# Seven products of a gated layer: four chained in one PSUM bank, weight work in smaller pieces and at other places

## The chip, the cores and the metric

The kernel runs on one core of a Trainium2 chip. The metric is device time in microseconds (us) of one execution. Five engines run their own instruction queues: TensorE multiplies into PSUM (eight banks), VectorE, ScalarE and GpSimd work on tensors in SBUF (here VectorE and ScalarE also read PSUM), and SyncE issues all DMA transfers of this kernel. In the profile they are PE (with PEld, its weight loads), DVE, ACT, POOL and SP.

## The reference

Inputs are fp32: q, k, v of shape (4, 8, 576, 64), decay factors f, and the five weights in float64, which the kernel converts itself by integer operations on the two 32-bit words of each.

```
def _attn_ref(q, k, v, f):                    # cut
    scores = q @ k.T / sqrt(D) + decay of f   # causal, softmax
    return softmax(scores) @ v
def _moe_ref(x, w_in, w_out) -> np.ndarray:   # 2304 x 512, d_ff 2048
    h = np.maximum(x @ w_in, 0.0)
    return (h * h @ w_out).astype(np.float32)
def _moe2_ref(x, w_gate, w_val, w_out):       # d_ff 1536
    gate = 1.0 / (1.0 + np.exp(-(x @ w_gate)))
    val = x @ w_val
    return (gate * val @ w_out).astype(np.float32)
```

The output of attention, heads side by side, goes through `_moe_ref` and then `_moe2_ref`.

## The kernel before

Every large product is made to fp32 accuracy from three TensorE passes: each operand is split into a high part (rounded to `F32R`) by ScalarE (a copy) and a low part (the rest) by VectorE or GpSimd (a subtraction); high x high, high x low and low x high add up in PSUM. Splitting costs ScalarE, VectorE and GpSimd much of their time.

The stages follow each other on TensorE:

1. Attention for 16 pairs of heads, 0 to 196 us. The change does not touch it.
2. Up stage, 196 to 390 us (L693 to L713): x times w_in, 96 groups of 12 matmuls (`up1`, L203), eight banks in turn; ScalarE squares, VectorE makes differences, and DMA stores ("spills", `g_spill`, L198) carry the results out of 14 tiles `gt` to DRAM. Beside it, weights are loaded and converted in "units" (L671 to L681), each in three phases a group apart: `conv_a` (ScalarE), `conv_b` (four VectorE instructions L141, L142, L145, L148), then a use. Six blocks of w_out2 are converted here too and stored to DRAM (`wo_d`). `load_units` (L685) issues the raw loads; there are two raw buffers, so load n + 2 needs the conversion of block n done.
3. w_out stage, 390 to 581 us (L863 to L925): seven products of block sums in place of eight block products, as 84 steps of 12 matmuls. Each step's operand comes back from DRAM (`d_load`) and is split (`d_split`, L664 and L665) two steps ahead. Gate and value blocks of the next stage's first unit are converted beside it (`D1W`). In its last block of products GpSimd makes sums of the result blocks (`t_sum`, L761, `t4_sum`) and ScalarE and VectorE split these (`t_hi`, `t_lo`).
4. Gate and value stage, 581 to 870 us (L1135 to L1146): six units of 256 columns, three pairs of token blocks each (`jj`), and for each pair a gate half and a value half. A half is again seven products (numbered 1 to 7; `product`, L961) of six matmuls of 384 columns. Four results come of them: 1 + 2, 1 + 6 + 5 + 3, 1 + 6 + 7 + 4 and 1 + 6 + 7 + 5. `post` (L988) empties the banks: ScalarE copies product 1, VectorE adds 6, 7, 5 (+3), 7 (+4) in turn into SBUF; products 2, 3 and 4 are accumulated by TensorE onto 1, 5 and 7. Gate results go through a sigmoid on ScalarE, value results are multiplied with them (`gated`) and stored to DRAM. Weights of the next unit are converted beside it; `slot` (L1044) says after which product. `w_sum` (GpSimd), `w_hi` (ScalarE) and `w_lo` (GpSimd, 512, 256 and 1024 columns) make the block sums and the split of a unit's weights.
5. Last stage, 870 to 1022 us (L1158 on): the gated values come back from DRAM and are multiplied with w_out2.

The whole order is written out by hand: inside `tc.manual_schedule()` each engine's queue has its instructions in the order in which the Python code issues them, each engine works its queue in that order, and semaphores make an instruction wait for the data or the buffer that it needs. So the places at which `at`, `D1X` or `TQ1` put a function set the order.

## Time and profile before

Three runs: 1025.5, 1025.58 and 1027.56 us, median 1025.58. The profiled execution took 1024.2 us; its span, from the first to the last instruction, is 1022.3.

| stage | from to, us | PE busy | DVE busy | ACT busy | POOL busy |
|---|---|---|---|---|---|
| up, to its last tenths | 196 to 386 | 190.0 of 190 | 123.2 | 116.4 | 22.4 |
| w_out, before its last block | 420 to 556 | 133.9 of 136 | 112.1 | 76.7 | 53.7 |
| w_out, last block | 556 to 581 | 21.3 of 25 | 19.5 | 10.0 | 18.2 |
| gate and value, start | 581 to 623 | 35.7 of 42 | 38.3 | 17.4 | 28.8 |
| gate and value, later | 623 to 765 | 135.1 of 142 | 117.1 | 45.1 | 54.5 |
| last | 890 to 1000 | 110.0 of 110 | 30.2 | 28.3 | 0.4 |

Matmuls overlap, so "busy" is the time in which at least one is under way; a stage can be 100% busy at different paces. The number of matmuls in a stretch shows the pace.

### The profile page before, as it was taken

The page shows a single profiled execution, that of the slowest core. Times are in us where ns is not written, and L with a number is a line of the kernel's source. Part 1 is how long each engine was busy: PE and PEld are TensorE (multiplying, and loading weights), DVE is VectorE, ACT ScalarE, POOL GpSimd, SP SyncE. Part 2 cuts the span into 40 slices and gives each one's busy share as a digit, 9 for nine tenths or more (in the row PEclk, how much of TensorE's full clock was granted, in tenths as well). Part 3 has the DMA queues.
Part 4 walks back from the last instruction along what each step waited for, and adds up shares of the span by engine and source line. Part 5 has one row for each costly group of instructions (what it writes and reads, how often), then busy time and mean ns, then how long its engine had stood idle before and what let it go on. Part 6 is the DMA issues. An engine that isn't in the chain of part 4 may idle for free. (4 is left out here: it accounts for less than half of the span.)

```text
span 1022.3 us, 16943 instructions
## 1 busy us (share of the span) xinstructions
PE 983.7 (96%) x5968; PEld 914.2 (89%) x5968; DVE 713.9 (70%) x1314; ACT 506.0 (49%) x1037; POOL 349.3 (34%) x403
## 2 busy tenths in 40 slices
PE   7999999999999998999999889999999999999998
PEld 5888878899999998999998779899999999788886
DVE  6878888356666676698788797978787788422221
ACT  6778878566566654554555433322322333322221
POOL 6776777211011122052066874433242322200000
PEclk9999999999999998999999989999999999999999
DMA  5444341177888888766665313223232324533442
GB/s 126 108 124 93 75 91 46 46 240 248 273 282 287 281 251 289 229 206 197 197 180 167 110 37 124 88 88 108 83 119 81 122 88 150 170 134 128 131 135 75
DMA packets 139220, 153.52 MB, mean 150 GB/s; under 512 B 65024, under 2 KB 116224, under 8 KB 139136
## 3 DMA queue, kind: packets, MB, share of 16 engines
q1 hardware_dynamic: 139136, 152.45, 48.7%
q8 instruction: 47, 0.77, 0.3%
q14 instruction: 37, 0.30, 0.1%
HBM read 98.77 MB, written 53.62 MB: 149 GB/s over the span
## 5 line engine op out<-in xcount | busy, mean ns | idle before, releaser
L209 PE MATMUL ps<-xT,hl 128*128 128x384 f32 x1104 | 191.6, 335 | 0.0
L209 PEld LDWEIGHTS ps<-xT,hl 128*128 128x128 f32 x1104 | 191.5, 188 | 0.0
L919 PE MATMUL ps<-gg,ao 128*128 128x384 f32 x1008 | 181.7, 339 | 9.7 <-DVE gg L665 5.9
L919 PEld LDWEIGHTS ps<-gg,ao 128*128 128x128 f32 x1008 | 177.0, 190 | 14.3 <-DVE gg L665 9.9
L665 DVE TENSOR_TENSOR gg<-gl,gg 128x768 fp32r<-128x768 f32 x84 | 94.8, 1139 | 38.7 <-ACT gg L664 38.2
L462 POOL TENSOR_TENSOR pt<-pt,sm 128x128 f32<-128x128 f32 (+2 forms) x142 | 104.3, 766 | 49.1 <-DVE sm L454 43.1
L968 PE MATMUL ps<-xT,r 128*128 128x384 f32 x576 | 114.2, 341 | 3.8 <-POOL r L827 2.8
L968 PEld LDWEIGHTS ps<-xT,r 128*128 128x128 f32 x576 | 102.9, 189 | 4.6 <-POOL r L827 3.1
L664 ACT ACTIVATE gg<-gl 128x768 fp32r<-128x768 f32 x84 | 70.7, 843 | 70.5 <-DMA gl<-g 51.7
L195 DVE TENSOR_TENSOR gt<-gt 128x384 f32<-128x384 f32 x96 | 52.3, 586 | 64.8 <-ACT gt L218 60.0
L359 ACT ACTIVATE pt<-pt,nm 128x128 f32<-128x128 f32 (+1 forms) x144 | 82.5, 583 | 11.2 <-DVE nm L351 11.2
L169 POOL TENSOR_TENSOR hl<-wf,hl 128x512 fp32r<-128x512 f32 x16 | 20.7, 1292 | 161.4 <-ACT hl L165 161.4
L1173 PE MATMUL ps<-f,t 128*128 128x512 f32 x324 | 75.4, 389 | 0.0
L1173 PEld LDWEIGHTS ps<-f,t 128*128 128x128 f32 x324 | 60.8, 188 | 12.6
L1016 ACT ACTIVATE sg<-sg 128x384 f32<-128x384 f32 x33 | 17.4, 526 | 104.2 <-DVE sg L982 103.3
L351 DVE CUSTOM_DVE_ANT_0 pt<-pa,maskc 128x128 f32<-128x128 f32 (+2 forms) x144 | 66.7, 513 | 2.3 <-PE pa L373 2.1
L1125 DVE TENSOR_TENSOR t<-gl,t 128x768 fp32r<-128x768 f32 x24 | 24.4, 1017 | 58.9 <-ACT t L1120 58.9
L968 PE MATMUL ps<-t,r 128*128 128x384 f32 x288 | 57.4, 340 | 5.7 <-DVE sg L982 3.6
L145 DVE SCALAR_TENSOR_TENSOR wtmp<-wraw,wtmp 128x512 int32<-128x512 int32 x68 | 61.3, 901 | 2.0
L982 DVE TENSOR_TENSOR sg<-ps,sg 128x384 f32<-128x384 f32 x94 | 51.8, 553 | 14.7 <-ACT sg L992 5.7
L124 ACT ACTIVATE wtmp<-wraw 128x512 f32<-128x512 f32 x68 | 44.8, 661 | 34.3 <-DMA wraw<-in_moe_w_out_dram 23.8
L968 PE MATMUL ps<-xT,f 128*128 128x384 f32 x288 | 59.1, 342 | 0.0
(180 smaller groups left out, 1804.7 us busy)
## 6 DMA issues: line engine op xcount, KB each, us to landing
gl<-g SPq DMA_DIRECT2D x120, 384.0 KB
g<-gt SPq DMA_DIRECT2D x168, 192.0 KB
wraw<-in_moe_w_out_dram SPq DMA_DIRECT2D x28, 512.0 KB
g<-sg SPq DMA_DIRECT2D x43, 192.0 KB
wraw<-in_moe_w_in_dram SPq DMA_DIRECT2D x16, 512.0 KB
wraw<-in_moe_w_gate_dram SPq DMA_DIRECT2D x12, 512.0 KB
wraw<-in_moe_w_val_dram SPq DMA_DIRECT2D x12, 512.0 KB
g<-pb SPq DMA_DIRECT2D x29, 192.0 KB
```

Of the source, the lines that this page charges most:

```text
L145: lambda: nc.vector.scalar_tensor_tensor(out=xi, in0=hi, scalar=-0x40000000, in1=xi, op0=ALU.bitwise_and, op1=ALU.bitwise_or),
L195: nc.vector.tensor_tensor(out=t, in0=a, in1=b_, op=ALU.subtract)
L209: nc.tensor.matmul(h, lhsT=a, rhs=xT[c][:, b_, t0:t0 + BT], start=(c == 0 and i == 0), stop=(c == KD - 1 and i == 2))
L351: nc.vector.tensor_tensor_reduce(out=o, in0=s, in1=mask, scale=1.0, scalar=3.0e38, op0=ALU.add, op1=ALU.min, accum_out=nm_t[p % 2][:, c:c ...
L359: nc.scalar.activation(out=x, in_=x, func=AF.Exp, bias=nm_t[p % 2][:, c:c + 1], scale=-1.0, accum_out=sm_t[p % 2][:, c:c + 1])
L462: nc.gpsimd.tensor_tensor(out=x, in0=x, in1=sm_t[p % 2][:, c:c + 1].to_broadcast([128, e - a]), op=ALU.mult)
L664: nc.scalar.activation(out=s[:, 0], in_=t, func=AF.Copy)
L665: nc.vector.tensor_tensor(out=s[:, 1], in0=t, in1=s.bitcast(F32)[:, 0], op=ALU.subtract)
L919: nc.tensor.matmul(o, lhsT=ws[:, a, u, cs], rhs=s[:, b_, u, :], start=(k_ in (0, 2, 5) and w == u == x == 0), stop=(w == NW - 1 and u == 1 ...
L968: nc.tensor.matmul(o, lhsT=w[p][:, a, ws], rhs=operand(n, jj, b_, c), start=(n not in (2, 3, 4) and c == x == 0), stop=(c == 1 and x == 2) ...
L982: nc.vector.tensor_tensor(out=out, in0=a, in1=b, op=ALU.add)
L1173: nc.tensor.matmul(o, lhsT=s[:, a, t, cs], rhs=w[b_], start=(u == t == x == 0), stop=(u == NU2 - 1 and t == 1 and x == 2),)
```

## The change

- In the up stage two gate and two value blocks are converted and stored to DRAM in place of the six w_out2 blocks, and come back with `x_load` in the w_out stage. `load_units` is called in phase 2 instead of phase 1. Of w_out2, seven blocks are now converted about the last unit of the gate and value stage, four in its units 1 to 4 (stored, then reloaded), one in the last stage.
- In the w_out stage `t_sum` works on halves (one of two column blocks, 384 columns) and sums, weight splits and block splits stand at other steps (`D1X`). The table of the sigmoid is loaded there by a one-element sigmoid (`warm`).
- In the gate and value stage, products 1, 6, 5 and 3 accumulate in one bank without a break: ScalarE copies the bank after 1, after 6 and after 5, and after 3 it holds the second result. Product 2 has its own bank, 7 and 4 share one. VectorE adds 2 to the copy after 1, (7 + 4) to the copy after 6, and 7 to the copy after 5. Products 3 and 4 of a half are issued in the next half. Sigmoids and the sum with 7 are put into the queues a product later (`todo2`, `follow`).
- A weight's low part on GpSimd comes in pieces of 256 columns, and the fourth piece is new (`w_piece`); first-unit pieces of value and the second unit's gate go to VectorE. `slot` spreads conversion instructions over eight positions of the 14 products of a pair.
- In the last stage two groups of its matmuls stand between the last two products; buffers come from memory freed by the weights.

```diff
...
-        if 1 <= u <= M2 - NE:
-            us.append(("out2", NE + u - 1))
+        if 1 <= u <= 4:
+            us.append((("gate", 0), ("gate", 1), ("val", 0), ("val", 1))[u - 1])
...
             elif ph == 1:
...
+            else:
                 load_units(min(n + 3, NX))
...
-    def t_sum(n, jj):
-        p1, u2, u3 = (pu[n, jj] for n in range(3))
+    def t_sum(n, jj, c):
+        p1, u2, u3 = (pu[i, jj][:, c, :] for i in range(3))
...
+        for b in range(s.start, s.stop, 256):
+            v = slice(b, b + 256)
+            nc.gpsimd.tensor_tensor(
+                out=t[:, 1, v], in0=x[:, b - s.start:b - s.start + 256], in1=t.bitcast(F32)[:, 0, v], op=ALU.subtract
+            )
...
+    for n, (key, m) in enumerate((("gate", 0), ("gate", 1), ("val", 0), ("val", 1))):
+        dx(14 + 4 * n, part_fn(x_load, key, m))
+    for x in range(4):
+        dx(33 + 4 * x, part_fn(w_sum, "gate", 0, x))
+        dx(K6 + 4 if x < 2 else K6 + 5, part_fn(w_sum, "val", 0, x))
+    for x in range(4):
+        dx(K6 + x, part_fn(w_hi, "gate", 0, x))
+        dx(K6 + 1 + x, part_fn(w_lo, "gate", 0, x, nc.vector))
+    dx(K6 + 7, warm)
+    for x in range(6):
+        dx(K6 + 5 + x // 2, part_fn(t_sum, x // 2, 0, x % 2))
+        dx(K6 + 8 + x // 2, part_fn(t_sum, x // 2, 1, x % 2))
...
+    for x, n in enumerate((1, 2, 3)):
+        dx(K6 + 9 + x, part_fn(t_hi, n, 0))
...
-    BANK = {1: 0, 2: 0, 6: 1, 5: 2, 3: 2, 7: 3, 4: 3}
+    BANK = {1: 0, 6: 0, 5: 0, 3: 0, 2: 1, 7: 2, 4: 2}
...
+    def post(key, u, jj, n):
+        o = obank(key, n)
+        if n in (1, 6, 5):
+            t = keep[key, n] = sg()
             nc.scalar.activation(out=t, in_=o, func=AF.Copy)
...
+        if n == 5:
+            t, d = keep.pop((key, 5)), obank(key, 7)
+
+            def c22():
+                add(t, d, t)
+                finish(key, u, jj, 3, t)
+
+            todo2.append([1, c22])
+        elif n in (2, 4):
+            t = keep.pop((key, 1 if n == 2 else 6))
             add(t, o, t)
+            finish(key, u, jj, 0 if n == 2 else 2, t)
+        elif n == 3:
+            if key == "gate":
+                sigm(1, sg(), o)
             else:
+                gated(u, jj, 1, o, keep[1])
+
+    def follow():
+        n = len(todo2)
+        for x in todo2[:n]:
+            x[0] -= 1
+        for x in todo2[:n]:
+            if x[0] < 0:
+                x[1]()
+                todo2.remove(x)
...
-        return u + s // 24, s // 8 % 3, (0, 0, 1, 6, 6, 7, 7, 8)[s % 8]
+    def slot(s):
+        return s // 24, s // 8 % 3, (0, 2, 3, 5, 7, 9, 10, 12)[s % 8]
...
-                seq = [(key, u, jj, n) for n in (1, 6, 7, 5)] + due + [(key, u, jj, 2)]
-                due = [(key, u, jj, n) for n in (4, 3)]
+                x = [(key, u, jj, n) for n in (1, 2, 6, 7, 5)]
+                seq = x[:2] + due[:1] + x[2:4] + due[1:] + x[4:]
+                due = [(key, u, jj, n) for n in (3, 4)]
...
+    for c, x in enumerate(due):
+        down(0, c)
+        follow()
+        product(*x)
+        post(*x)
...
```

TensorE, one gate half of a later unit, before: the operands name the product (`xT` the input's blocks, `t` block sums, `f` and `r` the weights of two keys), and `ps` with its number the bank; products 1, 6, 7, 5, then 4 and 3 of the value half ahead, then 2.

```order
L968 MATMUL ps_2715<-xT_113,r_6556 128x384 x3
L968 MATMUL ps_2715<-xT_114,r_6556 128x384 x3
L968 MATMUL ps_2716<-t_2_6736,r_6556 128x384 x6
L968 MATMUL ps_2718<-t_2_6714,r_6556 128x384 x6
L968 MATMUL ps_2717<-xT_113,r_6556 128x384 x3
L968 MATMUL ps_2717<-xT_114,r_6556 128x384 x3
L968 MATMUL ps_2714<-t_1_6552,r_6889 128x384 x6
L968 MATMUL ps_2713<-xT_115,r_6889 128x384 x3
L968 MATMUL ps_2713<-xT_116,r_6889 128x384 x3
L968 MATMUL ps_2715<-xT_115,r_6556 128x384 x3
L968 MATMUL ps_2715<-xT_116,r_6556 128x384 x3
```

The same place now: products 1, 2, the other half's 3, then 6, 7, the other half's 4, then 5.

```order
L987 MATMUL ps_2719<-xT_117,r_6891 128x384 x3
L987 MATMUL ps_2719<-xT_118,r_6891 128x384 x3
L987 MATMUL ps_2720<-xT_119,r_6891 128x384 x3
L987 MATMUL ps_2720<-xT_120,r_6891 128x384 x3
L987 MATMUL ps_2722<-xT_119,f_6277 128x384 x3
L987 MATMUL ps_2722<-xT_120,f_6277 128x384 x3
L987 MATMUL ps_2719<-t_2_6759,r_6891 128x384 x6
L987 MATMUL ps_2721<-t_2_6792,r_6891 128x384 x6
L987 MATMUL ps_2724<-t_1_6521,f_6278 128x384 x6
L987 MATMUL ps_2719<-xT_117,r_6891 128x384 x3
L987 MATMUL ps_2719<-xT_118,r_6891 128x384 x3
```

Bank 2719 now comes back after two other products each time (1, 6, 5), where each of 1, 6, 7 and 5 had a bank of its own.

GpSimd at the start of the w_out stage's last block of products, before: sums of a value block (L808, `wt`), block sums of 768 columns (L761), then the operations of `t4_sum` on the first pair (L767, L768).

```order
L808 TENSOR_TENSOR wt<-wtmp 128x256 x2
L808 TENSOR_TENSOR wt<-wt,wtmp 128x256
L808 TENSOR_TENSOR wt<-wtmp,wt 128x256
L761 TENSOR_TENSOR pa_4914<-pa_4914,pa_4912 128x768
L761 TENSOR_TENSOR pa_4912<-pa_4912,pa_4910 128x768
L761 TENSOR_TENSOR pa_4910<-pa_4914,pa_4910 128x768
L767 TENSOR_TENSOR pa_4912<-xT_115,pa_4910 128x384
L768 TENSOR_TENSOR pa_4912<-pa_4912,xT_115 128x384
```

And now, from the same value sums on (L815), with the block sums at L768.

```order
L815 TENSOR_TENSOR wt<-wx 128x256 x2
L815 TENSOR_TENSOR wt<-wt,wx 128x256
L815 TENSOR_TENSOR wt<-wx,wt 128x256
L768 TENSOR_TENSOR pa_4900<-pa_4900,pa_4898 128x384 x2
L768 TENSOR_TENSOR pa_4898<-pa_4898,pa_4896 128x384 x2
L768 TENSOR_TENSOR pa_4896<-pa_4900,pa_4896 128x384 x2
```

Six sums of 384 columns stand where three of 768 stood; the next pair's six follow before the operations of `t4_sum`, and the low parts of the value weights, which came after those on GpSimd, are VectorE's.

SyncE at the end of the up stage, before: stores of results (L201), raw loads (L115), the first operands of the w_out stage (L658).

```order
L115 DMA wraw<-in_moe_w_out_dram 128x1024
L201 DMA g_3_61<-gt 128x384 x4
L115 DMA wraw<-in_moe_w_out_dram 128x1024
L658 DMA gl<-g_0_58 128x768
L658 DMA gl<-g_1_59 128x768
L658 DMA gl<-g_2_60 128x768
L201 DMA g_3_61<-gt 128x384
L700 DMA wo_73<-wtmp 128x512
L201 DMA g_3_61<-gt 128x384 x16
```

And now, with the stores at L204, raw loads at L118 and operands at L661.

```order
L118 DMA wraw<-in_moe_w_out_dram 128x1024
L204 DMA g_3_61<-gt 128x384 x4
L661 DMA gl<-g_0_58 128x768
L661 DMA gl<-g_1_59 128x768
L661 DMA gl<-g_2_60 128x768
L204 DMA g_3_61<-gt 128x384
L118 DMA wraw<-in_moe_w_out_dram 128x1024
L204 DMA g_3_61<-gt 128x384 x16
```

The last raw load stands behind the first operands now, and no store of a converted block (L700) is left here.

## Rows read from the trace of the kernel before

**Rows 1.** The page's busy times: us (share of the span) xinstructions.

```profile
PE 983.7 (96%) x5968; PEld 914.2 (89%) x5968; DVE 713.9 (70%) x1314; ACT 506.0 (49%) x1037; POOL 349.3 (34%) x403
```

**Rows 2.** Busy time by stretch: length, then each engine's us (xinstructions), clock, DMA.

```profile
196.00:386.00 190.00, 190.00 (x1097) 190.00 (x1096) 123.19 (x229) 116.38 (x232) 22.38 (x17) 1.00 0.81 259
390.00:392.00 2.00, 0.00 (x0) 0.00 (x0) 1.76 (x3) 1.94 (x5) 1.87 (x2) 1.00 1.07 397
392.00:420.00 28.00, 26.19 (x134) 25.94 (x135) 17.82 (x20) 12.36 (x18) 5.29 (x3) 0.88 0.82 267
420.00:556.00 136.00, 133.92 (x762) 131.66 (x762) 112.11 (x129) 76.70 (x114) 53.71 (x36) 1.00 0.65 190
556.00:581.00 25.00, 21.25 (x115) 19.40 (x114) 19.50 (x20) 9.95 (x14) 18.24 (x12) 1.00 0.50 152
581.00:623.00 42.00, 35.66 (x179) 33.91 (x178) 38.25 (x49) 17.42 (x31) 28.80 (x21) 0.92 0.15 49
623.00:765.00 142.00, 135.09 (x760) 132.65 (x759) 117.08 (x181) 45.13 (x89) 54.48 (x49) 1.00 0.31 99
765.00:830.00 65.00, 63.61 (x362) 63.28 (x362) 51.68 (x81) 20.62 (x41) 20.20 (x17) 1.00 0.28 92
830.00:870.00 40.00, 39.20 (x220) 38.26 (x219) 35.21 (x58) 14.78 (x29) 10.31 (x8) 1.00 0.41 142
870.00:890.00 20.00, 18.73 (x82) 14.83 (x81) 9.09 (x13) 7.14 (x11) 6.19 (x4) 1.00 0.61 197
890.00:1000.00 110.00, 110.00 (x487) 91.09 (x486) 30.15 (x33) 28.28 (x37) 0.36 (x1) 1.00 0.42 136
```

**Rows 3.** What TensorE waited for, whole span: us in total, times, longest us.

```profile
PE ps L968 <- DVE sg L982: 7.1, 5, 2.6
...
PE ps L919 <- DVE gg L665: 5.9, 11, 1.2
...
PE ps L968 <- POOL r L827: 2.8, 1, 2.8
```

**Rows 4.** The same of SyncE's queue, 196 to 396.

```profile
SPq L115 <- DVE wf L148: 41.7, 15, 5.6
```

**Rows 5.** The same of ScalarE, 196 to 396.

```profile
ACT gt L217 <- DMA g<-gt: 3.4, 1, 3.4
```

**Rows 6.** Timeline, 566 to 574: start, us, engine, line [idle <-releaser].

```profile
566.28 6.26 POOL L761 TENSOR_TENSOR pa<-pa,pa 128x768 f32<-128x768 f32 x3
...
568.15 0.84 ACT L782 ACTIVATE f<-pa 128x768 fp32r<-128x768 f32 x1 [3.70 <-POOL pa L761]
...
570.75 2.61 DVE L790 TENSOR_TENSOR f<-pa,f 128x768 fp32r<-128x768 f32 x1
```

**Rows 7.** Groups by form, gate stage (fourth: up stage): xcount | busy, mean ns.

```profile
L982 DVE TENSOR_TENSOR sg<-ps,sg 128x384 f32<-128x384 f32 x94 | 51.8, 553 | 14.7 <-ACT sg L992 5.7 <-PE ps L968 4.5 <-DVE sg L982 0.5
...
L992 ACT ACTIVATE sg<-ps 128x384 f32<-128x384 f32 x22 | 10.5, 478 | 0.6 <-PE ps L968 0.6
...
L145 DVE SCALAR_TENSOR_TENSOR wtmp<-wraw,wtmp 128x512 int32<-128x512 int32 x26 | 30.5, 1173 | 0.7
...
L145 DVE SCALAR_TENSOR_TENSOR wtmp<-wraw,wtmp 128x512 int32<-128x512 int32 x35 | 24.2, 693 | 1.2
...
L827 POOL TENSOR_TENSOR r<-wt,r 128x1024 fp32r<-128x1024 f32 x7 | 18.1, 2581 | 13.4 <-ACT r L823 13.1
...
L808 POOL TENSOR_TENSOR wt<-wtmp 128x256 f32<-128x256 f32 x24 | 19.1, 815 | 49.4 <-DVE wtmp L148 46.4 <-DVE f L827 3.0
```

**Rows 8.** Timeline, 708 to 717, gate stage.

```profile
708.18 2.77 POOL L827 TENSOR_TENSOR f<-wt,f 128x1024 fp32r<-128x1024 f32 x1 [4.38 <-ACT f L823]
...
708.62 2.88 DVE L148 SCALAR_TENSOR_TENSOR wtmp<-wraw,wtmp 128x512 int32<-128x512 int32 x1
...
713.67 1.88 DVE L982 TENSOR_TENSOR sg<-ps,sg 128x384 f32<-128x384 f32 x3
...
716.93 0.53 ACT L1016 ACTIVATE sg<-sg 128x384 f32<-128x384 f32 x1 [7.52 <-DVE sg L982]
```

More of the change, by code (lines that the diff above doesn't have):

```diff
@@ L80 @@
     NU2 = M2 // 2
-    wo_d = [dram.tile([128, 512], F32, name=f"wo_{m}") for m in range(M2)]
+    w_d = {
+        x: dram.tile([128, 512], F32, name=f"w_{x[0]}_{x[1]}")
+        for x in [(key, m) for key in ("gate", "val") for m in range(2)] + [("out2", m) for m in range(M2)]
+    }
     g2_d = [[dram.tile([128, 2, BT], F32, name=f"g2_{u}_{j}") for j in range(6)] for u in range(NU2)]
@@ L968, in product @@
                 nc.tensor.matmul(
-                    o, lhsT=w[p][:, a, ws], rhs=operand(n, jj, b_, c), start=(n not in (2, 3, 4) and c == x == 0),
-                    stop=(c == 1 and x == 2), skip_group_check=n in (2, 3, 4),
-                )
-        return o
-    keep = {}
+                    o, lhsT=w[p][:, a, ws], rhs=operand(n, jj, b_, c), start=(first and c == x == 0),
+                    stop=(c == 1 and x == 2), skip_group_check=not first,
+                )
+    keep, todo2 = {}, []
     def sg():
@@ L1068 @@
+        pos(7 + c, part_fn(t4_sum, 1, c, nc.gpsimd))
+        pos(27 + 2 * c, part_fn(t4_sum, 2, c, nc.vector))
+        for n in range(3):
+            pos(10 + 2 * n + c, part_fn(t_sum, n, 2, c))
+    def slot(s):
+        return s // 24, s // 8 % 3, (0, 2, 3, 5, 7, 9, 10, 12)[s % 8]
     wo = {}
@@ L1083, in o_lo, with o_store @@
         nc.gpsimd.tensor_tensor(out=wo[m][1], in0=cf[m], in1=wo[m][0].bitcast(F32), op=ALU.subtract)
+    def o_store(m):
+        nc.sync.dma_start(out=w_d["out2", m], in_=cf.pop(m))
     def o_load(m):
[L1086 to L1099 removed]
@@ L1100 @@
-    for m in (6, 7):
-        at(NU2 - 1, 2, 5 + 4 * (m - 6), part_fn(o_hi, m), part_fn(o_lo, m), part_fn(o_load, m + 2))
+        t = raw_p.tile([128, 1024], F32, tag="raw", name="wraw")
+        cf[m] = t[:, 0:512]
+        nc.sync.dma_start(out=cf[m], in_=w_d["out2", m])
+    items, mo = [], NE
+    for u in range(NU2):
+        z = 24 * u + (6 if u == 0 else 0)
+        if u == NU2 - 1:
+            items += [(z - 4 + 4 * m, "out2", m) for m in range(NE)]
+            continue
+        for n, key in enumerate(("gate", "val")):
+            items += [(z + 8 * n + 4 * i, key, 2 * u + 2 + i) for i in range(2)]
+        for i in range(min(u, 1)):
+            items.append((z + 16 + 4 * i, "out2", mo))
+            mo += 1
@@ L1119, in e_hi @@
             gg[i] = egg[i % 3]
-            nc.scalar.activation(out=gg[i][:, 0], in_=gl[i], func=AF.Copy)
+            if i > 1:
+                nc.scalar.activation(out=gg[i][:, 0], in_=gl[i], func=AF.Copy)
+                return
+            for c in range(2):
+                nc.scalar.activation(out=gg[i][:, 0, c], in_=gl[i][:, c], func=AF.Copy)
     def e_lo(i):
@@ L1125, in e_lo @@
             nc.vector.tensor_tensor(out=s[:, 1], in0=gl.pop(i), in1=s.bitcast(F32)[:, 0], op=ALU.subtract)
+    for i in range(3):
+        at(NU2 - 1, 2, (1, 2, 7)[i], part_fn(e_load, i))
     for i in range(2):
[L1128 removed]
         at(NU2 - 1, 2, 7 + 3 * i, part_fn(e_hi, i))
         at(NU2 - 1, 2, 9 + 3 * i, part_fn(e_lo, i))
[L1132 to L1133 removed]
+    for x in items[:2]:
+        w_load(*x[1:])
     due = [None, None]
@@ L1161 @@
         e_lo(i + 2)
-        if 8 <= i + 8 < M2:
-            o_hi(i + 8)
-            o_lo(i + 8)
-            o_load(i + 10)
-        s = gg.pop(i)
-        for c in range(3):
-            o = bank(2 + 3 * (j % 2) + c)
-            cs = slice(c * 128, (c + 1) * 128)
-            for t in range(2):
-                w = wo[2 * u + t]
-                for x, (a, b_) in enumerate(((0, 0), (0, 1), (1, 0))):
-                    nc.tensor.matmul(
-                        o, lhsT=s[:, a, t, cs], rhs=w[b_], start=(u == t == x == 0),
-                        stop=(u == NU2 - 1 and t == 1 and x == 2),
-                    )
+        if i < len(rest):
+            m = rest[i]
+            if m == M2 - 1:
+                o_conv0(m)
+                while todo:
+                    one()
+            o_hi(m)
+            o_lo(m)
+            if i + 2 < len(rest):
+                o_load(rest[i + 2])
+        for c in range(2 if i == 0 else 0, 3):
+            o = down(i, c)
             if u == NU2 - 1:
```

248 lines of the change are left out of this document (112 added, 136 removed).

## The prediction, made before the changed kernel was run

> **What bounds the kernel now.** I read the page's busy shares first: TensorE is busy for 983.7 of 1022.3 us [rows 1]. That share hides pace, so I cut the span into stages and counted matmuls per stretch [rows 2]. The stretch 196 to 386 runs without a gap: 1097 matmuls of 384 columns in 190.0 us, 0.1732 us each. That is the pace against which I measure the stages that the change touches; a stretch's loss is its length less its matmuls times 0.1732.
>
> - 390 to 420 (start of the w_out stage): 2.0 us with no matmul, then 28.0 - 134 x 0.1732 = 4.8; loss 6.8
> - 420 to 556: 136.0 - 762 x 0.1732 = 4.0
> - 556 to 581 (its last block of products): 25.0 - 115 x 0.1732 = 5.1
> - 581 to 623 (start of the gate and value stage): 42.0 - 179 x 0.1732 = 11.0
> - 623 to 765: 142.0 - 760 x 0.1732 = 10.4; 765 to 830: 2.3; 830 to 870: 1.9
> - 870 to 890 (start of the last stage): the pace there is that of 890 to 1000, 110.0 / 487 = 0.2259 us; 20.0 - 82 x 0.2259 = 1.5
>
> Together 43.0 us: all that a better order can win. Before 196 and after 890 nothing moves on TensorE, and 196 to 386 has no loss to win. The table of waits says who is late: mostly VectorE, whose adds empty PSUM (L982) or whose subtractions make operands (L665), once GpSimd's weight subtraction (L827) for 2.8 us [rows 3]. The granted clock adds to the loss: a mean of 0.88 in 392 to 420 and 0.92 in 581 to 623, part of each at the lower of its two levels (1.2 and 2.4 GHz) after TensorE stood, against 1.00 around them [rows 2].
>
> **The change, part by part.**
>
> *Raw loads a group later, w_out2 blocks out of the up stage.* In 196 to 396 SyncE's queue stands 41.7 us, up to 5.6 at a time, in front of a w_out load whose buffer VectorE's last conversion instruction still reads (L148) [rows 4]; the stores of results queue behind. Near the end ScalarE waits 3.4 us for a result tile that such a store must free [rows 5]; the operands of the w_out stage's first steps are behind it in ScalarE's queue, and TensorE stands at 390. Now the load is queued one group (12 matmuls, 2.08 us) after the conversion instead of with it. Four gate and value blocks take the place of six w_out2 blocks, so two 512 KB loads and two 256 KB stores leave this stretch, and none of the four falls in its last quarter; ScalarE and VectorE are busy 116.4 and 123.2 of 190.0 us there, which covers the conversions. If a late load instead makes ScalarE wait, eight PSUM banks of queued results stand before TensorE does. Bounds 0 to 6.8 us; I take 4.8, leaving 2.0, because DMA shows share 1.07 at 390 to 392 and the last steps' stores still burst. The first rows of the next stage need three loads of 384 KB, and they stay in the same place of the queue.
>
> *Conversions out of the w_out stage.* 16 VectorE instructions go from 400 to 556. GpSimd's four sums for a gate block are spaced by four steps instead of standing in front of an operand sum. Bounds 0 to 4.0; I take 2.0, since the operand sums of 512 columns that GpSimd and VectorE both touch stay as they are.
>
> *Block sums in half pieces, issued before their readers.* At 566.28 GpSimd takes 6.26 us for three sums of 768 columns; ScalarE, which has the next split in the same step, stands 3.70 us for the first; VectorE's subtraction of 128x768 beside it takes 2.61 us [rows 6]. Now the first reader on ScalarE stands three to four steps (over 6 us) behind its sums, and the chain on GpSimd up to the stage's end is 4 + 12 shorter sums: at 0.82 each for 256 columns [rows 7] and half of 2.09 for 384, 3.3 + 12.5 = 15.8 us, from 16.7 us (eight steps) before the end. The value weights' low parts, for which TensorE stood 2.8 us [rows 3], are made by VectorE instead, five and more products ahead of their use. Bounds 0 to 5.1 at 556 to 581; I take 3.6. For 581 to 623, 0 to 11.0; I take 7.5: it is the stage's start and all the operand preparation still falls into it.
>
> *Four products chained in one bank.* Per half (gate or value of one token pair, 36 in all) VectorE makes 3 sums instead of 5: 72 fewer, at 0.553 us [rows 7], 39.8 us. ScalarE makes 72 more copies at 0.478 us, 34.4 us, in a stage where it is busy 17.4 + 45.1 + 20.6 + 14.8 = 97.9 of 289 us [rows 2]; it ends near half busy. But VectorE (38.3 + 117.1 + 51.7 + 35.2 = 242.3 of 289 us) gets back five w_out2 conversions of four instructions in this stage, at most 0.693 to 1.173 each [rows 7], so 14 to 23 us, and about 5 us of weight and block sums that GpSimd had. It stays near 80 to 85% busy over a shorter stage. What changes is who waits. In the old order five conversion instructions stood together: VectorE was held from 708.62, where one took 2.88 us beside GpSimd's 2.77 us subtraction of 1024 columns, to 713.67, when three late sums start, and the sigmoid came at 716.93 [rows 8]. Now conversion instructions stand at eight separate positions per token pair, at most one per product, and 1024 columns on GpSimd become four pieces. TensorE needs, between links of the chain, one copy: two other products (12 matmuls, 2.08 us) lie between, and the copy takes 0.48.
>
> The price of the cut on GpSimd: one 1024-column piece at 2.58 becomes four of about 0.82 [rows 7], 3.3 us; at 54.5 busy of 142 that is covered.
>
> The conversion instruction of L145 takes 0.693 us in the up stage and 1.173 in the gate stage, where GpSimd works beside it [rows 7]. The Trainium skill (SBUF — State Buffer, "Who interferes with whom") says that a VectorE instruction with two SBUF inputs and a GpSimd instruction that reads SBUF exclude each other for a whole instruction, whoever issues first; the 2.88 beside 2.77 agrees. By that rule shorter pieces shorten each hold, but not their sum, and the cut would win lateness alone: the sum is the same as below.
>
> For 623 to 870 the bounds are 0 and 14.6 us; a loss here or in 581 to 623 is possible through ScalarE's queue alone, and is the second rival. The other terms take work off a queue or move it earlier, so their lower end is 0. If all of it ran as 765 to 830 does (2.3 us lost in 65), 247 x 2.3 / 65 = 8.7 would remain and 5.9 be won; with half that loss 10.2. I take 8.
>
> *Last stage.* Two groups of its matmuls stand between the last two products, and the third split buffer is free earlier: of 1.5 us I take 1.0; ends 0 and 1.5.
>
> **Sum.** 4.8 + 2.0 + 3.6 + 7.5 + 8.0 + 1.0 = 26.9 us. The profiled execution took 1024.2 us (span 1022.3 and 1.9 around it); 1024.2 - 26.9 = 997.3. The median of the runs shown, 1025.58, is 1.4 above the profiled one: 999.
>
> **Rivals.**
>
> *VectorE stays late (25%).* Its load hardly falls, as worked out. If lateness follows load, the gate stage from 581 wins 5 instead of 15.5 us, and the time is 999 + 10.5 = 1009. For it: the busy share. Against: the lump at 708 to 714 is order, not load, and 765 to 830 runs at 0.1796 us per matmul under the same share (51.7 of 65).
>
> *ScalarE's queue blocks the chain; slower (9%).* The sigmoid that follows product 2 waits for VectorE's sum and stands in front of the copy after product 6, which product 5 needs. From product 2's end to product 5 lie four products, 4.2 us at 1.05; less 0.53 for the sigmoid and 0.48 for the copy, VectorE's sum may end up to 3.2 us after its product. Beyond that TensorE waits. ScalarE's 7.52 us wait for VectorE at 716.93 [rows 8] shows that such lateness exists. If every half loses 1 us so, 36 us are added, the gate stage's 15.5 are not won, and the first 11.4 stay: 1025.6 - 11.4 + 36, less the 20 us of old stalls that these replace, about 1030. The Trainium skill (PSUM — Partial Sum Buffer, "Engine vs sequencer instructions") has ScalarE's queue as strictly in order; the row agrees, and by that rule this rival needs nothing but a late sum. I hold it unlikely because an add stands at most behind one conversion instruction now.
>
> *Nothing comes free (4%).* Each stall is replaced by another of its size, as DMA in 390 to 420 and operand work in 581 to 623 would have it: within 2 us of 1025.6.
>
> *Nearly all goes (7%).* Only 3 or 4 of the 43.0 us stay: 986.
>
> **How the numbers follow.** The forecast, 999 (992 to 1006 by its own terms), has 55%. A change of 0.2%, 2 us, is about what a measurement of this kernel can tell. Faster: 55 + 25 + 7, and a point of the slower rival, whose stalls may be smaller than the rest wins: 88%. Same: 4%. Slower: 8%. The range 988 to 1013 takes in the forecast with its bounds, most of the 1009 case, and leaves out the slower cases and most of the 986 case.
>
> **What would show it.** Right: 390 to 400 without a gap and at clock 1.00; SyncE no longer waiting for L148; no wait of ScalarE for block sums at the stage's end; matmul pace from 623 on under 0.179; VectorE sums 108 instead of 180, copies 108 instead of 36. Wrong: TensorE waiting for ScalarE's copies at the third or sixth product of a half, or the late VectorE sums still ending most of its waits, or a new wait for raw blocks by ScalarE in 196 to 386.

## The result, and the profile after

The changed kernel takes 1000.33 us (median of four runs, 1000.02 to 1000.61), the kernel before beside it 1026.57 (1025.5 to 1029.05): ratio 0.9741, 95% interval 0.9721 to 0.9761. The profiled executions are 24.0 us apart (1024.2 and 1000.19), where the prediction's sum was 26.9.

The page's busy times after [rows 1]: us, share of the span, instructions.

```profile
PE 975.2 (98%) x5968; PEld 911.2 (91%) x5968; DVE 663.2 (66%) x1254; ACT 544.2 (55%) x1124; POOL 353.6 (35%) x439
```

VectorE does 50.7 us less, ScalarE 38.2 more. Busy time by stretch after [rows 2], with the same columns; the borders follow the stages, which now end earlier (the w_out stage at 570.8 instead of 581.2).

```profile
386.00:388.00 2.00, 2.00 (x13) 2.00 (x13) 1.97 (x3) 0.94 (x3) 1.20 (x1) 1.00 0.57 206
...
390.00:392.00 2.00, 1.11 (x7) 1.08 (x7) 2.00 (x2) 1.90 (x4) 2.00 (x3) 1.00 0.54 148
392.00:420.00 28.00, 26.54 (x151) 25.81 (x150) 19.33 (x24) 13.58 (x19) 1.98 (x2) 1.00 0.72 214
420.00:548.00 128.00, 126.98 (x728) 125.70 (x727) 95.82 (x106) 69.05 (x99) 51.51 (x35) 1.00 0.67 193
548.00:572.50 24.50, 24.23 (x138) 23.59 (x137) 21.02 (x24) 14.71 (x23) 17.79 (x14) 1.00 0.59 172
572.50:614.50 42.00, 35.78 (x186) 34.01 (x185) 41.21 (x54) 20.50 (x42) 28.96 (x23) 0.92 0.17 54
614.50:750.00 135.50, 134.85 (x766) 134.20 (x765) 94.19 (x161) 64.99 (x135) 57.42 (x70) 1.00 0.37 121
750.00:815.00 65.00, 65.00 (x371) 65.00 (x371) 44.95 (x76) 32.58 (x67) 26.84 (x31) 1.00 0.39 128
815.00:846.00 31.00, 31.00 (x177) 30.91 (x176) 23.61 (x39) 16.06 (x34) 5.75 (x5) 1.00 0.45 150
846.00:866.00 20.00, 20.00 (x92) 16.84 (x91) 10.30 (x14) 7.41 (x12) 7.51 (x6) 1.00 0.59 193
```

With the pace of 0.1732 us per matmul the losses are these (in the last stretch 12 of the 92 matmuls are of the gate and value stage, 80 at the last stage's 0.2259; the "first 42 us" of the gate and value stage are 572.5 to 614.5 after, from 1.7 us into it):

| stretch | loss before | loss after | won | predicted |
|---|---|---|---|---|
| 390 to 420 | 6.8 | 30 - 158 x 0.1732 = 2.6 | 4.2 | 4.8 |
| w_out, middle | 4.0 | 1.9 | 2.1 | 2.0 |
| w_out, last block | 5.1 | 0.6 | 4.5 | 3.6 |
| gate and value, first 42 us | 11.0 | 42 - 186 x 0.1732 = 9.8 | 1.2 | 7.5 |
| gate and value, later | 14.6 | 2.8 + 0.7 + 0.3 = 3.8 | 10.8 | 8.0 |
| border to the last stage | 1.5 | 0 | 1.5 | 1.0 |

One trace stands behind each row. Where runs below leave a stage's order as it is in the changed kernel, their traces show how far executions differ: 180.2 to 182.7 us for the w_out stage, 272.9 to 274.8 for the gate and value stage. So a row is good to about 2 us.

The sum won is 24.3. One row is far off: the start of the gate and value stage hardly gained. Before, TensorE stood 2.8 us there for GpSimd's low part [rows 3] and 3.5 for VectorE's sums; both waits are gone, and others of the same size are there. What TensorE waited for after, 571 to 620 (total, times, longest, in us):

```profile
PE ps L987 <- DVE f L797: 4.2, 2, 3.4
PE ps L987 <- ACT f L789: 1.8, 1, 1.8
PE ps L987 <- ACT sg L1020: 0.3, 1, 0.3
```

The timeline of the same place after: start, length, engine, line, in brackets the idle time before and its releaser.

```profile
557.79 2.10 POOL L815 TENSOR_TENSOR wt<-wx 128x256 f32<-128x256 f32 x2 [5.80 <-ACT gg L667]
...
562.08 16.54 POOL L768 TENSOR_TENSOR pa<-pa,pa 128x384 f32<-128x384 f32 x12
...
582.82 1.19 POOL L775 TENSOR_TENSOR pa<-pa,xT 128x384 f32<-128x384 f32 x1
...
584.05 0.84 ACT L789 ACTIVATE f<-pa 128x768 fp32r<-128x768 f32 x1 [4.18 <-POOL pa L775]
584.94 0.44 PE L987 MATMUL ps<-f 128*128 128x384 f32 x1 [1.80 <-ACT f L789]
585.31 1.75 DVE L797 TENSOR_TENSOR t<-pa,t 128x768 fp32r<-128x768 f32 x1
586.98 1.75 DVE L797 TENSOR_TENSOR f<-pa,f 128x768 fp32r<-128x768 f32 x1
588.78 1.97 PE L987 MATMUL ps<-f 128*128 128x384 f32 x5 [3.40 <-DVE f L797]
```

GpSimd begins the four sums of a value block (L815) at 557.79, 13.0 us before the stage's end, after standing 5.8 us, and works from 562.08 for 16.54 us on twelve block sums (the first and the second token pair's), and only then makes the sums for product 4 of the first pair (L774, L775). ScalarE, then VectorE, then TensorE wait for these one after the other; after the 3.40 us TensorE runs some 13 matmuls at 320 ns, the lower clock level, and the stretch has a mean granted clock of 0.92.

### The profile page after: what moved, and what is told of

Read it like the earlier page. It is cut to its first block, busy times and chain, and to the rows that moved or that the text cites. A ratio compares the mean times of both kernels' runs of the same rounds, so it can differ in the third digit from the quotient of the medians.

```text
span 998.4 us, 16960 instructions
## 1 busy us (share of the span) xinstructions
PE 975.2 (98%) x5968; PEld 911.2 (91%) x5968; DVE 663.2 (66%) x1254; ACT 544.2 (55%) x1124; POOL 353.6 (35%) x439
## 4 chain that ended last, share of the span: by engine, by line
PE 82%; DVE 7%; ACT 3%; DMA 3%; issue 2%; POOL 2%; SPq 0%; ACTq 0%; DVEq 0%; POOLq 0%
PE ps L987 23%; PE ps L212 19%; PE ps L1204 15%; PE ps L934 10%; PE pa L510 4%; PE pa L376 4%; PE pa L476 3%; DMA gl<-g 2%; PE pa L340 2%; PE pa L447 1%; DVE gg L668 1%; DVE ao L653 1%; ACT gg L667 1%; PE pa L212 1%; PE pa L482 1%
## 5 line engine op out<-in xcount | busy, mean ns | idle before, releaser
L934 PE MATMUL ps<-gg,ao 128*128 128x384 f32 x1008 | 177.6, 335 | 3.6 <-DVE gg L668 3.4
L934 PEld LDWEIGHTS ps<-gg,ao 128*128 128x128 f32 x1008 | 174.5, 188 | 6.7 <-DVE gg L668 6.4
L987 PE MATMUL ps<-xT,r 128*128 128x384 f32 x576 | 110.5, 342 | 0.7 <-ACT sg L1020 0.4
L667 ACT ACTIVATE gg<-gl 128x768 fp32r<-128x768 f32 x84 | 70.9, 845 | 71.1 <-DMA gl<-g 38.0
L1020 ACT ACTIVATE sg<-ps 128x384 f32<-128x384 f32 x65 | 31.9, 491 | 55.2 <-PE ps L987 54.2
L220 ACT ACTIVATE gt<-ps 128x384 f32<-128x384 f32 x92 | 44.5, 484 | 27.3 <-PE ps L212 25.1
L1000 DVE TENSOR_TENSOR sg<-ps,sg 128x384 f32<-128x384 f32 x65 | 36.0, 556 | 34.9 <-PE ps L987 27.2
L127 ACT ACTIVATE wtmp<-wraw 128x512 f32<-128x512 f32 x68 | 45.0, 663 | 24.7 <-DMA wraw<-in_moe_w_out_dram 8.2
L987 PE MATMUL ps<-xT,f 128*128 128x384 f32 x288 | 57.4, 342 | 0.3 <-ACT sg L1020 0.3
L987 PE MATMUL ps<-t,r 128*128 128x384 f32 x288 | 54.7, 337 | 0.0
```

The source lines that it names most:

```text
L127: nc.scalar.activation(out=x, in_=rf[:, :, 1], func=AF.Abs)
L220: nc.scalar.activation(out=r, in_=uph.pop(g), func=AF.Relu)
L667: nc.scalar.activation(out=s[:, 0], in_=t, func=AF.Copy)
L934: nc.tensor.matmul(o, lhsT=ws[:, a, u, cs], rhs=s[:, b_, u, :], start=(k_ in (0, 2, 5) and w == u == x == 0), stop=(w == NW - 1 and u == 1 ...
L987: nc.tensor.matmul(o, lhsT=w[p][:, a, ws], rhs=operand(n, jj, b_, c), start=(first and c == x == 0), stop=(c == 1 and x == 2), skip_group_ ...
```

## The experiments

Theory at the outset: late raw loads took away the gap at 390; spread conversions, the chain (products 1, 6, 5 and 3 in one bank) and short GpSimd pieces together took the late VectorE sums away; the order on GpSimd's queue makes the new stall at 585. The rivals are in the expectations.

**Product 4's first sum ahead**, and the splits of the second and third pair some products later.

```diff
-        dx(K6 + 8 + x // 2, part_fn(t_sum, x // 2, 1, x % 2))
         ...
         dx(K6 + 11, part_fn(t4_sum, 0, c, nc.gpsimd))
+    for x in range(6):
+        dx(K6 + 11, part_fn(t_sum, x // 2, 1, x % 2))
...
-        (1, 1, 4, 6), (2, 1, 7, 9), (3, 1, 11, 13), (4, 1, 17, 19),
+        (3, 1, 9, 11), (1, 1, 11, 13), (2, 1, 13, 15), (4, 1, 20, 22),
...
-        pos(7 + c, part_fn(t4_sum, 1, c, nc.gpsimd))
+        pos(14, part_fn(t4_sum, 1, c, nc.gpsimd))
...
```

> The changed kernel, with one thing moved: GpSimd makes the two sums for product 4 of the first token pair before the six sums of the second pair, and the splits of the second and third pair stand a few products later in the order that follows. Theory (order on GpSimd's queue): the changed kernel's two waits at 584.94 (1.95 us) and 588.78 (3.66 us), and the slow matmuls until about 593.5, come from product 4's sum standing behind twelve others (16.54 us). Then both go, the loss of the 42 us at the start of the gate and value stage falls from 9.8 to about 4, and the time from 1000.3 to 993.5-996. Rival (too much operand work at the stage's start for ScalarE and VectorE, whatever the order): the wait moves to an operand of the second pair, the loss stays above 8, and the time is 999-1002.

Measured: 996.88 us (996.32 to 997.3), ratio 0.9706 (0.9683 to 0.9729), 3.5 us under the changed kernel. First 42 us and the stretch after:

```profile
572.50:614.50 42.00, 36.02 (x193) 33.53 (x194) 41.69 (x56) 21.84 (x44) 29.09 (x23) 1.00 0.19 62
614.50:750.00 135.50, 135.34 (x771) 135.02 (x771) 94.76 (x162) 64.90 (x136) 57.56 (x70) 1.00 0.37 123
```

The clock stays at 1.00 and no wait is over 1.7 us. But the loss is still 42 - 193 x 0.1732 = 8.6, not 4: VectorE is busy 41.7 of 42 and ends 4.2 us of smaller waits, ScalarE 1.6. The long stall was order, as the theory has it. The size of the theory's win was wrong: the loss stays above 8, as the rival said, and the time lies between the ranges of the two. Of the 3.5 us the table's measure finds 1.2 in these 42 us.

**Second unit's gate blocks out of the stage's start**, without and with the edit above.

```diff
-        if 1 <= u <= 4:
-            us.append((("gate", 0), ("gate", 1), ("val", 0), ("val", 1))[u - 1])
+        if u <= 5:
+            us.append((("gate", 0), ("gate", 1), ("val", 0), ("val", 1), ("gate", 2), ("gate", 3))[u])
...
+    for i in range(2):
+        pos(2 * i, part_fn(x_load, "gate", 2 + i))
```

> The changed kernel with the two gate blocks of the second unit converted in the up stage (its six blocks now in units one to six of eight) and read back from DRAM at the start of the gate and value stage, so that eight conversion instructions, some 8 to 9 us of VectorE, leave the first 42 us of that stage, where VectorE is busy 41 of 42. The order of the sums and splits is that of the changed kernel. Theory (too much work on VectorE there is what keeps the stage's start lossy): TensorE's two long waits shrink to under 2 us together, the clock stays up, loss 4 to 5 instead of 9.8, time 994-996.5; less 0 to 1 for the block that now falls late in the up stage. Rival (GpSimd's order, the sum for product 4 behind twelve others, decides): the waits at 585 and 589 stay within 1 us of 5.6 together, 999-1001.

> Both: product 4's first sum ahead on GpSimd as in the first run of this series, and the two gate blocks of the second unit converted in the up stage. Theory (order on GpSimd and load on VectorE each cost part of it): the start of the gate and value stage loses 3 to 4 us instead of 8.6, time 991-993.5. Rival (one of the two suffices, or the load is only moved to the up stage's end): no better than 996.9 by more than 1, 995.9-998.

Measured: 1003.97 us without (1001.32 to 1005.18; ratio 0.9789, 0.9773 to 0.9806), 999.26 with (0.9737, 0.9722 to 0.9751). Both are slower than either expectation allowed. The same stretch, first without, then with:

```profile
572.50:614.50 42.00, 35.77 (x186) 34.29 (x186) 33.45 (x45) 20.09 (x39) 29.12 (x24) 0.92 0.07 24
```

```profile
572.50:614.50 42.00, 38.11 (x211) 36.19 (x210) 37.57 (x46) 21.79 (x42) 32.59 (x27) 1.00 0.09 33
```

Without the first edit VectorE is busy 33.5 of 42 instead of 41.2, and TensorE waits as long as in the changed kernel, to the tenth of a microsecond:

```profile
PE ps L987 <- DVE f L797: 4.2, 2, 3.4
PE ps L987 <- ACT f L789: 1.8, 1, 1.8
```

So load alone is not the cause of the long stall. With both edits the loss is 42 - 211 x 0.1732 = 5.5, and the whole stage, up to the first group of the last stage, runs from 575.13 to 844.48, 269.4 us, against 570.75 to 845.5, 274.8, in the changed kernel; with the first edit alone it takes 272.4, with this one alone 273.6. So once the order is right, load is the next limit. The total is no better than with the first edit alone. Six blocks instead of four are now converted in the up stage; TensorE waits 2.1 us at 391.8 and 3.4 at 395.6, and 390 to 420 loses 30 - 127 x 0.1732 = 8.0, where the first edit alone loses 3.2. Without the first edit, in the same up stage, the profiled execution loses 4.2 there. It is the fastest of its four, only 1.1 us above the changed kernel's; the other 2.5 us of the median are in no trace. All six blocks in the first five units, with both edits, was not tried.

**Further moves of the splits**: product 4's first split earlier, the third pair's sums ahead of the second pair's product-4 sum, the third pair's splits in another order. The diff is against the first run of this series.

```diff
-    pos(8, part_fn(t_hi, 4, 0))
-    pos(10, part_fn(t_lo, 4, 0))
+    pos(6, part_fn(t_hi, 4, 0))
+    pos(8, part_fn(t_lo, 4, 0))
...
-        pos(14, part_fn(t4_sum, 1, c, nc.gpsimd))
+        pos(17, part_fn(t4_sum, 1, c, nc.gpsimd))
...
-            pos(15 + 2 * n + c, part_fn(t_sum, n, 2, c))
+            pos(11 + 2 * n + c, part_fn(t_sum, n, 2, c))
```

> The changed kernel with product 4's first sum moved ahead on GpSimd as in the first run of this series, and beyond it: the low part of product 4's operand stands on VectorE ahead of three adds, GpSimd makes the third pair's sums before the second pair's product-4 sum, and the splits of the third pair follow in the order in which their sources are free. Theory (the remaining waits at 584.87, 1.4 us, and 608.62, 1.9 us, are order in VectorE's and GpSimd's queues): both go, 993-995. Rival (VectorE is full from 570 to 615, and a split that is moved ahead makes another one late): 996-998.

Measured: 998.74 us (0.974, 0.9726 to 0.9755), a miss: the two waits are gone, and others of 1.6 and 2.4 us stand at 590.7 and 593.5, the second for a split of the second pair. Such new waits are what the rival said, but the time lies beyond its range too. The first 42 us:

```profile
572.50:614.50 42.00, 37.62 (x201) 36.13 (x200) 41.73 (x54) 20.88 (x41) 30.22 (x23) 0.96 0.17 54
```

Here the loss falls from 8.6 to 7.2, and the whole stage takes 271.9 us instead of 272.4. What is lost lies in front of it: the w_out stage, which has the same instructions in both runs, took 182.7 us in this trace and 180.2 in the other. So whether these moves cost or gain is not settled.

**Old order of the products, all else changed.** `SLOT`, `BANK`, `post` and the product sequence are those of before.

```diff
-                x = [(key, u, jj, n) for n in (1, 2, 6, 7, 5)]
-                seq = x[:2] + due[:1] + x[2:4] + due[1:] + x[4:]
-                due = [(key, u, jj, n) for n in (3, 4)]
+                seq = [(key, u, jj, n) for n in (1, 6, 7, 5)] + due + [(key, u, jj, 2)]
+                due = [(key, u, jj, n) for n in (4, 3)]
```

> The changed kernel with the products of a half in their order of before, with the banks and the emptying of before (five VectorE sums per half instead of three, one copy instead of three) and without the two groups of the last stage between the last products; the spread conversions, the short GpSimd pieces and the late raw loads stay. Theory (what the chain takes from VectorE's path to TensorE is worth most of the gate and value stage's 11.6 us): late VectorE sums end TensorE's waits again, 6 to 10 us come back in that stage and 1 in the last, time 1007-1012. Rival (spreading the conversions over eight positions is what did it): the sums come in time in the old order too, time 1000-1004.

Measured: 1003.54 us (0.9773, 0.9745 to 0.9801), 3.2 more than the changed kernel. Two later stretches of the stage:

```profile
614.50:750.00 135.50, 135.00 (x768) 134.68 (x768) 106.33 (x196) 49.96 (x99) 59.01 (x70) 1.00 0.36 118
750.00:815.00 65.00, 65.00 (x371) 65.00 (x370) 49.57 (x93) 24.23 (x48) 26.57 (x31) 1.00 0.40 128
```

VectorE has 12.1 us more to do from 614.5 to 750 (106.3 against 94.2), and TensorE does as many matmuls (768 against 766). The rest is at the borders: 1.9 us of standing at 850.9, where the two groups of the last stage that this edit also takes out stood, and 177 matmuls instead of 186 in the first 42 us. So with the conversions spread the chain as such is worth little; the rival was right.

**Conversions in lumps, all else changed.**

```diff
-        return s // 24, s // 8 % 3, (0, 2, 3, 5, 7, 9, 10, 12)[s % 8]
+        return s // 24, s // 8 % 3, (0, 0, 1, 7, 7, 8, 8, 9)[s % 8]
```

> The changed kernel with the conversion instructions of the gate and value stage in lumps, at the positions 0, 0, 1, 7, 7, 8, 8, 9 of the 14 products of a pair instead of 0, 2, 3, 5, 7, 9, 10, 12. Theory (the chain tolerates a late VectorE, since only copies of ScalarE stand between its links): TensorE hardly notices, 1000-1003. Rival (the spreading is what did it): five conversion instructions of 0.7 to 1.2 us stand in VectorE's queue before a sum, products wait for their bank, and 5 to 9 us of the stage's 11.6 come back, 1005-1010.

Measured: 1011.46 us (0.9847, 0.9823 to 0.9871), 11.1 more than the changed kernel, beyond even the rival's range; the theory (the chain makes TensorE indifferent) falls. First what VectorE waited for, 572 to 870, then the worst place:

```profile
DVE wtmp L144 <- ACT wtmp L127: 11.2, 14, 2.3
```

```profile
584.49 0.84 ACT L789 ACTIVATE f<-pa 128x768 fp32r<-128x768 f32 x1 [4.18 <-POOL pa L775]
585.24 0.65 ACT L127 ACTIVATE wtmp<-wraw 128x512 f32<-128x512 f32 x1
...
585.92 0.85 DVE L144 TENSOR_SCALAR wtmp<-wtmp 128x512 f32<-128x512 f32 x1 [2.31 <-ACT wtmp L127]
586.69 1.01 DVE L1000 TENSOR_TENSOR sg<-ps,sg 128x384 f32<-128x384 f32 x2
...
587.38 0.66 PE L987 MATMUL ps<-f 128*128 128x384 f32 x1 [3.80 <-DVE sg L1000]
```

The first conversion instruction (L144) needs ScalarE's copy (L127). In the changed kernel the copy is issued one of the eight positions ahead, one or two products; with this table it falls on the same product for half of the blocks, as here. So the edit does two things: it makes lumps, and it takes that distance away. ScalarE is held by GpSimd's late sum, VectorE by ScalarE, the sums behind L144 by VectorE, and TensorE by the bank that they must empty. The changed kernel shows no such wait of L144 among VectorE's waits of that stretch; the kernel before has 10.0 us of it. TensorE also waits 4.2 us in the stage for ScalarE's copies of the banks (L1020), up to 1.6 at a time.

Of the 11.1 us, 4.8 fall in the first 42 us (158 matmuls, loss 14.6 instead of 9.8). Later:

```profile
614.50:750.00 135.50, 133.89 (x752) 130.62 (x751) 95.59 (x162) 62.68 (x134) 54.54 (x68) 1.00 0.35 115
750.00:815.00 65.00, 63.92 (x363) 62.96 (x362) 43.14 (x75) 29.74 (x64) 24.80 (x32) 1.00 0.38 125
```

With 0.9 from 815 to 846 (174 matmuls) and 1.7 from there to the stage's end at 857.4 (56) the loss is 5.3 + 2.1 + 0.9 + 1.7 = 10.0, more than the changed kernel's 3.8 and less than the 14.6 of the kernel before. So with lumps, too, other parts of the change win some 5 us of the later stage. Whether it is the chain was not separated: the chain alone, in the kernel before, was not run.

**The table of positions alone, in the kernel before.**

```diff
-        return u + s // 24, s // 8 % 3, (0, 0, 1, 6, 6, 7, 7, 8)[s % 8]
+        return u + s // 24, s // 8 % 3, (0, 2, 3, 5, 7, 9, 10, 12)[s % 8]
```

> The kernel before with one thing of the change: the conversion instructions of the gate and value stage at the positions 0, 2, 3, 5, 7, 9, 10, 12 of the 14 products of a pair instead of 0, 0, 1, 6, 6, 7, 7, 8. Theory (the spreading is most of what the gate and value stage won, as the two runs of the changed kernel with the old products, 3.2 us, and with lumps, 11.1 us, say): the stage takes 278 to 281 us instead of 288.7, ratio 0.990 to 0.993. Rival (with five VectorE sums per half VectorE is full, and the spreading helps only together with the chain or with short pieces on GpSimd): 0.996 to 1.000.

Measured: ratio 0.9928 (0.9904 to 0.9953), 1017.71 us. The stage takes 279.9 us (584.15 to 864.03) instead of 288.7. Two stretches [rows 2]:

```profile
581.00:623.00 42.00, 35.21 (x180) 33.60 (x178) 38.28 (x48) 16.75 (x29) 32.88 (x22) 0.92 0.15 49
623.00:765.00 142.00, 141.18 (x801) 140.48 (x801) 113.51 (x190) 48.46 (x92) 53.31 (x50) 1.00 0.32 105
```

From 623 to 765 there are 801 matmuls instead of 760, a loss of 142 - 801 x 0.1732 = 3.3 instead of 10.4, with VectorE busy 80% of it (82% before). This one line is 8.8 us of the stage's gain; the first 42 us gain nothing from it. In both kernels the copy (L124) and the first conversion instruction (L141) stand at one and the same product, so here the spreading acts alone. VectorE's wait for the copy in the whole stage, first before, then with the table:

```profile
DVE wtmp L141 <- ACT wtmp L124: 10.0, 11, 1.2
DVE wtmp L141 <- ACT wtmp L124: 5.9, 8, 1.2
```

More than half of that wait stays, while TensorE's waits for VectorE's sums from 640 on fall from 9.0 to 1.6 us. So the lump behind the wait hurt more than the wait itself.

**Long GpSimd pieces, all else changed.**

```diff
-        for b in range(s.start, s.stop, 256):
-            ...
+        nc.gpsimd.tensor_tensor(out=t[:, 1, s], in0=x, in1=t.bitcast(F32)[:, 0, s], op=ALU.subtract)
```

> The changed kernel with GpSimd's work in long pieces again: a weight's low part in 512, 256 and 1024 columns, the block sums of the first and later pairs in 768 columns. Theory (a long GpSimd instruction holds VectorE's next instruction back for as long as it runs, and that makes it late): VectorE instructions of 2 us and more beside them, 3 to 6 us lost, 1003-1006, most of it at 556-623. Rival (GpSimd and VectorE share the same sum of time whatever the pieces, and TensorE no longer depends on VectorE within 2 us): within 1.5 us of 1000.3.

Measured: 1000.22 us (0.9738, 0.9713 to 0.9763), the changed kernel's time. VectorE's L148 from 623 to 840, first with long pieces, then in the changed kernel (xcount, busy, mean ns, idle):

```profile
L148 DVE SCALAR_TENSOR_TENSOR wtmp<-wraw,wtmp 128x512 int32<-128x512 int32 x26 | 24.0, 924 | 0.4
```

```profile
L148 DVE SCALAR_TENSOR_TENSOR wtmp<-wraw,wtmp 128x512 int32<-128x512 int32 x26 | 18.3, 702 | 0.4
```

The holds are there (the longest L148 takes 2.24 us beside long pieces, 0.76 beside short ones), and they cost TensorE nothing. The cut into pieces was not part of the gain.

**Raw loads early, in the changed kernel; raw loads late, in the kernel before.**

```diff
             elif ph == 1:
...
-            else:
                 load_units(min(n + 3, NX))
             if ph < 2:
```

```diff
             elif ph == 1:
...
+            if ph == 2:
                 load_units(min(n + 3, NX))
```

> The changed kernel with the raw weight loads of the up stage queued in phase 1 again, one group of 12 matmuls earlier, with the conversion instead of after it. Theory (SyncE's stand before the conversion's last instruction is what kept TensorE waiting at 390 before the change): SyncE waits over 60 us for VectorE's L148 and L151 in 196 to 396 again, ScalarE waits for a result tile at the stage's end, and 3 to 5 us come back at 390 to 420; 1003-1005. Rival (what helped there is that the two last units of loads and four transfers are gone from the up stage's end): no wait at 390, 1000-1001.

> The kernel before with one thing of the change: the raw weight loads of the up stage are queued one group later (phase 2); the six w_out2 blocks stay in this stage. Theory (the place of the loads decides): the two gaps at 390 to 400 shrink to 1 us each and 3 to 5 us are won, ratio 0.995 to 0.997. Rival (the number of blocks near the stage's end decides): the gap of 2.0 us with no matmul stays, ratio 0.999 to 1.001.

Measured: 999.57 us (0.9746, 0.9732 to 0.9761) and ratio 1.0017 (1.0 to 1.0033): on both sides the loads' place is worth nothing. What SyncE's queue waited for in 196 to 396, first with early loads, then in the changed kernel:

```profile
SPq L118 <- DVE wf L151: 28.3, 9, 5.1
SPq L113 <- DVE wf L151: 27.3, 12, 4.0
```

```profile
SPq L113 <- DVE wf L151: 24.4, 12, 3.2
SPq L118 <- DVE wf L151: 20.6, 9, 3.8
```

So early loads wait 55.6 us for VectorE's L151, late ones 45.0, and TensorE starts the w_out stage alike (155 and 158 matmuls from 390 to 420).

**Blocks at the end of the up stage**: two more in the changed kernel; the six of the kernel before in earlier units.

```diff
-        if 1 <= u <= 4:
+        if 1 <= u <= 6:
```

```diff
-        if 1 <= u <= M2 - NE:
-            us.append(("out2", NE + u - 1))
+        for x in ((0,), (1, 2), (3,), (4,), (5,), (), (), ())[u]:
+            us.append(("out2", NE + x))
```

> The changed kernel with two more weight blocks (gate 2 and 3) loaded, converted and stored in the last quarter of the up stage, as the kernel before had two w_out2 blocks there; their stored values are not used, so this is work in addition. Theory (the blocks that no longer fall near the up stage's end, and their two loads of 512 KB and stores of 256 KB, are what took the gap at 390 away; the place of the loads was not, as two runs showed): DMA share stays above 1.0 to 392, TensorE stands 2 to 4 us more at 390 to 400 with some 3 us at the lower clock, 1003-1006. Rival (the gap went for another reason, the order of the queues at the border of the stages): within 1 us of the changed kernel, 999.5-1001.5.

> The kernel before with the six w_out2 blocks of the up stage in its first five of eight units (one each, two in the second) instead of units two to seven: the same work, none of it in the last quarter. Theory (blocks near the stage's end make the gap at 390): 390 to 420 loses 2 to 3 us instead of 6.8 and keeps the higher clock, 3 to 5 us won, ratio 0.995 to 0.997. Rival (the gap depends on something else): ratio 0.999 to 1.001.

Measured: 1005.64 us (0.9806, 0.9791 to 0.982), 5.3 more; and ratio 0.9964 (0.9952 to 0.9976), 3.7 us less than before. With two more blocks:

```profile
390.00:392.00 2.00, 0.60 (x4) 0.28 (x2) 1.90 (x5) 1.94 (x6) 0.00 (x0) 1.00 1.03 377
392.00:420.00 28.00, 23.91 (x123) 23.66 (x124) 20.20 (x22) 12.74 (x19) 7.09 (x4) 0.88 0.66 207
```

The gap is back, with DMA at share 1.03 and the clock at 0.88, as before the change [rows 2]: loss 30 - 127 x 0.1732 = 8.0 against 2.6. In the other run the profiled execution shows less than its times: 390 to 420 loses 30 - 141 x 0.1732 = 5.6 instead of 6.8, at a clock of 0.94, and that execution is the slowest of its six; where the rest of its 3.7 us comes from stays open. So it is the blocks, not the place of the loads. Their number and their place are not separated, and the gap differs between executions: the two runs with the second unit's gate blocks share one up stage, and their traces lose 4.2 us with DMA at share 0.50 in 390 to 392, and 8.0 with DMA at 1.01.

## Why the prediction held, and where it failed

- **Start of the w_out stage (4.8, measured 4.2).** The size held, the cause did not. The step gave the win to the later raw loads and SyncE's 41.7 us in front of them [rows 4]; with L110's 19.9 they were 61.6 us, fell only to 45.0, and were harmless. The win came from what the same step named second, the blocks: fewer of them, and none in the stage's last quarter. Which of the two counts was not separated.
- **w_out, middle and last block (2.0 and 3.6, measured 2.1 and 4.5).** The sizes came out within what one trace can tell. ScalarE's wait of 3.70 us for the block sums [rows 6] is a wait of 2.44 at 570.43 now. Long sums gave the same time, so it is not the half pieces; that the earlier place of the sums and the 16 instructions fewer did it is argued, not shown.
- **Start of the gate and value stage (7.5, measured 1.2).** This step failed, and the term that failed is GpSimd's chain of 4 + 12 sums: 15.8 us, from 16.7 us before the w_out stage's end, so done 0.9 us before it. It began 13.0 us before the end and took 20.8 us (557.79 to 578.62), so it was done 7.9 us behind it. The twelve alone took 16.54, at 1.38 us each instead of half of 2.09. The wait of 5.8 us in front of the chain was in no term; the trace puts it down to ScalarE (L667), but the one buffer of `wt` was also read by VectorE (L836) until 557.65, and which it was is not shown. The step also stopped at the stage's end and did not follow product 4's sum, behind the twelve, to its reader. With the step's own figures that would have shown no stall: product 4's operand ready some 7 us into the stage (an estimate: 5.4 for its sums and 2.6 for its splits in the trace after, less 0.9), where TensorE asks for it 12.4 us in. So the sizes decided. Moving that sum ahead took the stall away and 3.5 us of the time; taking eight conversion instructions from VectorE, busy 41 of 42, brought the loss of these 42 us from 8.6 to 5.5. The 5.5 that stay are not explained further.
- **Gate and value stage, later (8.0, measured 10.8).** Right that it was order and not load: 8.8 us come with one table of positions, and with VectorE as busy as before. "What changes is who waits" gave the chain a part that it did not need: with the conversions spread, the old order of the products loses as little here (3.4 against 3.8). With lumps the chain did not make TensorE indifferent either (10.0 lost). What stood in VectorE's queue [rows 8] was more than slow instructions: the first of each block waited for ScalarE's copy, 10.0 us in the stage, 11 times. That the change also issues this copy one position earlier was not named.
- **Rivals.** *VectorE stays late* fell for the later stage; in the first 42 us VectorE is a limit beside the order on GpSimd. *ScalarE's queue blocks the chain* did not come: TensorE's waits for copies (L1020) total 0.6 us from 620 on. Its mechanism exists, though: with the conversions in lumps these waits are 4.2 us. *Nothing comes free* holds for one stretch of six.
- **The pages.** By the rule of the Trainium skill (SBUF — State Buffer, "Who interferes with whom") the prediction expected that shorter pieces shorten VectorE's holds and leave their sum. The longest hold did get shorter (L148 takes at most 2.24 us beside long pieces, 0.76 beside short). The sum of holds is in no view by itself: from 614.5 to 750 VectorE's busy time is 103.2 us beside long pieces and 94.2 beside short ones, GpSimd's 51.7 and 57.4. So VectorE's time did fall, and GpSimd paid part of it back; neither reached TensorE.

The time came out 1.3 us above the forecast, and that is partly luck: the sum of wins was 2.6 us short (6.3 too much at the stage's start, 2.8 too little behind it, 0.9 too little in the other stretches together). The forecast also added 1.4 us because the profiled execution before was that much faster than the median; in the changed kernel the two differ by 0.1, which hides 1.3 of the 2.6.
